# A gated linear-attention kernel with a two-matrix MLP: two tokens to a partition, one logarithm for both, quarter-tile scores and a written-out order

## The chip, the cores and the metric

The kernel runs on one core of a Trainium2 chip. A core has five engines that run beside each other and meet through semaphores: TensorE (PE, matrix products into PSUM), VectorE (DVE), ScalarE (ACT, functions from tables), GpSimd (POOL) and SyncE (SP), which here only issues transfers. Sixteen DMA engines move the data. PSUM has eight banks; only TensorE writes products to it, and VectorE and ScalarE read it.

The metric is the device time of one launch in microseconds. The kernel before takes 228.28 us (median of three runs, 227.02 to 230.74).

## The reference

For each of 4 batches and 8 heads a 48 x 48 state decays by a gate for each token and takes in an outer product. The outputs of the heads side by side, 3072 tokens of 384 numbers, then go through two matrices with a smooth gate between them:

```python
f = 1.0 / (1.0 + np.exp(-f_logit))
for t in range(S):                       # S = 768, head_dim 48
    state = f[:, :, t, :, None] * state + np.einsum('bhd,bhe->bhde', k[:, :, t], v[:, :, t])
    y[:, :, t] = np.einsum('bhd,bhde->bhe', q[:, :, t], state)
x = y.transpose(0, 2, 1, 3).reshape(3072, 384)
h = x @ w_in                             # 384 x 2048
g = 0.5 * (h + np.sqrt(h * h + 4.0))
out = g @ w_out                          # 2048 x 384
```

q, k, v, f_logit and the weights come as float32 in HBM, and the result is float32.

## The kernel before

The work goes in 24 chunks of 128 tokens, two chunks making a pair of 256 tokens; there are 12 pairs, three to a batch. A token is a partition. Each chunk is loaded by a transfer of its own, whose contiguous runs are the 48 floats of one token and head, 192 bytes:

```python
for r in range(x, y):                                   # the chunks of a pair
    nc.sync.dma_start(out=T[name, p][:, r],
        in_=src_of[name][b][:, c * C:(c + 1) * C, :].rearrange("h t d -> t h d"))
```

The product of gates up to a token is the exponential of a running sum. ScalarE takes exp(-f) and ln(1 + e), both over all 768 numbers of a partition (2 chunks x 8 heads x 48). The result is split into a high and a low half-precision part, TensorE sums both over the tokens with a triangular matrix `wcent`, and ScalarE takes two exponentials for each chunk. GpSimd or VectorE then multiplies q and k by them:

```python
nc.scalar.activation(out=f, in_=f, func=AF.Exp, scale=-1.0)                    # 128 x 768
nc.scalar.activation(out=T["ls", p][:, x:y], in_=..., func=AF.Ln, bias=1.0)    # 128 x 768
...                                                     # lhi = half(ls), llo = half(ls - lhi)
nc.tensor.matmul(out=ca, lhsT=wcent, rhs=lhi[...][:, r, :, 0:D], start=True, stop=False)
nc.tensor.matmul(out=ca, lhsT=wcent, rhs=llo[...][:, r, :, 0:D], start=False, stop=True)
...                                                     # sums at the chunk's ends: 16 small products
nc.scalar.activation(out=T[name, p][:, r]..., in_=T["ca", p, r][:, 0:H * D], func=AF.Exp, scale=sign)
eng.tensor_tensor(out=qk[...][:, x:y, i, :, 0:D], in0=T[name, p][:, x:y], in1=T[e, p][:, x:y], op=ALU.mult)
```

q and k are transposed for each chunk, by TensorE for pairs 0 to 4 and by the DMA for pairs 5 to 11. Scores, mask, output and state of a chunk follow:

```python
nc.tensor.matmul(out=T["sc", r, s][:, j, :], lhsT=qkT[o:o + D, NP + j, :], rhs=qkT[o:o + D, j, :],
                 start=True, stop=True)                 # 8 a chunk, 48 rows x 128 columns, over 128
nc.vector.tensor_tensor(out=T["pm", r][:, s], in0=T["sc", r, s], in1=mask16..., op=ALU.mult)
nc.tensor.matmul(out=y[:, j], lhsT=T["qkT", r][:, j, :], rhs=T["sn", r][:, j], ...)
nc.tensor.matmul(out=y[:, j, s], lhsT=T["pm", r][:, s, j, :], rhs=T["v16", p][:, i, 2 * j + s, :], ...)
...                                                     # state: u = old state + k^T v, then times gam
```

y is copied to half precision and transposed to `xT`. The MLP of a pair is 48 products of 256 columns (M1, into the tile hps) with a square, a root and a gate between them, and 32 products of 384 columns (M2, into o):

```python
nc.tensor.matmul(out=hb[:, a, :], lhsT=w_in16[j2][:, j, a * 128:(a + 1) * 128], rhs=T["xT", p][:, j, :], ...)
nc.scalar.activation(out=T["hsq", p, j4][:, a], in_=T["h", p, j2], func=AF.Square, scale=1.0)
nc.scalar.activation(out=T["r16", p, j4], in_=T["hsq", p, j4], func=AF.Sqrt, scale=0.25, bias=1.0)
nc.vector.scalar_tensor_tensor(out=T["g", p]..., in0=T["h", p, 2 * j4 + a], scalar=0.5, in1=T["r16", p, j4][:, a],
                               op0=ALU.mult, op1=ALU.add)
nc.tensor.matmul(out=T["o", p, i], lhsT=T["g", p][:, jn, i * C:(i + 1) * C], rhs=w_out16[jn // 2][:, jn % 2, :], ...)
nc.sync.dma_start(out=out[t0:t0 + C, :], in_=T["o_sb", p, i])
```

Exp and ln lie in one table of ScalarE and sqrt in another, so a change from one kind of work to the other loads a table. The order of all instructions is made at build time by a list scheduler (`Plan`) from priorities in the source. PSUM is split into three fixed rings: five banks for hps, two for everything of the attention, one for o. The copy of o leaves through a ring of two `o_sb` buffers.

Of the kernel before, what the change touches and what calls it, by code (L numbers as in the profile page):

```python
# [15 lines left out]
GROUPS = [[0], [1], [2], [3], [4], [5, 6], [7, 8], [9, 10], [11]]  # L16

XBAR = [5, 6, 7, 8, 9, 10, 11]

BASE = {  # L20
    "A": [-91.5, -48.2, -86.7, 59.5, 5.1, 3.6, 35.4, 93.4, 55.3, 161.2, 112.5, 128.2],
    "B": [-33.0, -23.9, 18.0, -28.5, -32.3, 71.1, -18.2, 43.6, 49.9, 25.6, 129.6, 106.7],
    "M": [63.0, -3.2, -1.9, 48.3, 21.6, 51.8, 114.9, 66.8, 229.7, 86.1, 210.4, 238.2],
    "O": [63.2, 45.4, 128.9, 46.1, 124.2, 143.7, 179.0, 123.5, 212.6, 237.4, 202.6, 191.4],
}
PART = {n: k for k, v in {
    "A": "W hi lo qk v16 nls gam", "B": "T SC KV Y Yc YT xq xy", "M": "M1 M R G", "O": "M2 ev out"}.items()
    for n in v.split()}

SHIFT = {  # L30
    "ld": 25.6, "win": 4.5, "wout": 7.0, "W": -4.7, "hi": 73.7, "lo": -32.1, "qk": -11.9, "v16": -32.1,
    "nls": -54.3, "gam": -112.9, "T": -87.4, "xq": -171.2, "SC": 9.3, "Y": -140.2, "Yc": 36.7, "YT": 70.6,
    "xy": 89.2, "KV": 58.5, "M1": 3.8, "M": 94.0, "R": -53.7, "G": -57.6, "M2": 33.2, "ev": -104.7,
    "out": 212.9,
}

NEAR = {'PE': 0.02, 'ACT': 0.1, 'DVE': 0.05, 'POOL': 0.3, 'SP': 0.2}

ENG = {
    "hi": "DDDDPDPPPPPP",  # L40
    "lo": "PPPDPPPDPPPD",
    "qk": "PPPPDPDDPDPP",
    "v16": "PDPPDPPPPPPP",
    "T": "DDADDDDDDDAAADDADDADDDDD",
    "Yc": "AADDADDDDDDDDDADDDDDDDDD",
    "ev": "DDDDDADDDDDDDADADAADAAAA",
}
FULL = {"D": "DVE", "A": "ACT", "P": "POOL"}

FINE = [0]  # L50

START = {"POOL": 3.8, "DVE": 3.6, "PE": 3.4, "ACT": 0.7, "SP": 0.7}

AFTER = {'in': 0, 'out': 2}


NH, NA, NO = 5, 2, 1

WDMA, VDMA = True, False

ORDER = "P0 P1 i03 f2 i47 o07 qkv2"


class Op:
    __slots__ = ("eng", "dur", "deps", "emit", "due", "allocs", "uses", "end", "kind", "dma", "ins", "flow", "issued")

    def __init__(self, eng, dur, emit, deps=(), due=0.0, allocs=(), uses=(), kind=None, dma=None, ins=()):
        self.eng, self.dur, self.emit, self.due, self.kind, self.dma = eng, dur, emit, due, kind, dma
        self.deps = [d for d in deps if d is not None]
        self.allocs, self.uses = list(allocs), list(uses)  # L70
        for b in self.uses:
            b.users.append(self)
        self.end = None
        self.ins = list(ins)
        self.flow = None


class Ring:
    def __init__(self, n, ordered):
        self.n, self.bufs, self.ordered, self.made = n, [], ordered, 0  # L80


class Buf:
    def __init__(self, ring):
        self.ring, self.users = ring, []
        self.seq = ring.made
        ring.made += 1


class Plan:  # L90

    HOP = 0.22
    TABLE = 1.3

    def __init__(self):
        self.queues = {}
        self.order = []

    def add(self, queue, eng, dur, emit, p=None, at=None, due=0.0, **kw):
        if isinstance(dur, dict):
            eng = FULL[ENG[queue][p if at is None else at]]
            dur = dur[eng]
        due += SHIFT.get(queue, 0.0) + (0.0 if p is None else BASE[PART[queue]][p])
        op = Op(eng, dur, emit, due=due, **kw)
        self.queues.setdefault((eng, queue), []).append(op)
        return op

    def ready(self, op):  # L110
        t = 0.0
        for d in op.deps:
            if d.end is None:
                return None
            t = max(t, d.end + (0.0 if d.eng == op.eng and d.dma is None else self.HOP))
        for b in op.allocs:
            r = b.ring
            k = len(r.bufs) - r.n
            if r.ordered and b.seq != len(r.bufs):
                return None  # L120

            k += sum(1 for x in op.allocs[:op.allocs.index(b)] if x.ring is r)
            if k >= 0:
                for u in r.bufs[k].users:
                    if u.end is None:
                        return None
                    t = max(t, u.end + (0.0 if u.eng == op.eng and u.dma is None else self.HOP))
        return t

    def flows(self):  # L130


        todo = {"SP": [], "POOL": []}
        for op in self.order:
            if not isinstance(op, str) and op.dma is not None:
                todo[op.eng].append([op.issued, op.dma[0], op])
        t = 0.0
        while todo["SP"] or todo["POOL"]:
            live = {e: q[0] for e, q in todo.items() if q and q[0][0] <= t + 1e-9}
            later = [q[0][0] for e, q in todo.items() if q and e not in live]  # L140
            if not live:
                t = min(later)
                continue
            rate = {"SP": 0.35, "POOL": 0.65} if len(live) == 2 else {e: 1.0 for e in live}
            step = min([x[1] / rate[e] for e, x in live.items()] + [a - t for a in later])
            t += step
            for e, x in live.items():
                x[1] -= step * rate[e]
                if x[1] <= 1e-9:
                    x[2].flow = t + x[2].dma[1] - x[2].issued  # L150
                    todo[e].pop(0)

    def run(self, passes=3):
        for n in range(passes):
            for ops in self.queues.values():
                for op in ops:
                    op.end = None
                    for b in op.uses + op.allocs:
                        b.ring.bufs = []
            self.order = []  # L160
            self.once()
            if n + 1 < passes:
                self.flows()

    def once(self):
        heads = {k: 0 for k in self.queues}
        free = dict(START)
        dma_free = 0.0
        table = None
        left = sum(len(v) for v in self.queues.values())  # L170
        by_eng = {}
        for k in self.queues:
            by_eng.setdefault(k[0], []).append(k)
        stretch = None
        loose = False
        while left:
            best = None
            for eng, ks in by_eng.items():
                now = free.get(eng, 0.0)
                cands = []  # L180
                for k in ks:
                    if heads[k] < len(self.queues[k]):
                        op = self.queues[k][heads[k]]
                        t = self.ready(op)
                        if t is not None:
                            cands.append((max(now, t), op, k))
                if not cands:
                    continue
                if eng == "PE" and stretch is not None and not loose:

                    if any(heads[k] < len(self.queues[k]) and self.queues[k][heads[k]].kind == ("W", stretch)
                           for k in ks):
                        cands = [c for c in cands if c[2][1] != "M1" or not c[1].allocs]
                        if not cands:
                            continue
                if eng == "ACT" and stretch is None and not loose:

                    opened = []
                    for c in cands:
                        if c[1].kind is not None and c[1].kind[0] == "W":  # L200
                            ins = [d for o in self.queues[c[2]][heads[c[2]]:heads[c[2]] + 16]
                                   if o.kind == c[1].kind for d in o.ins]
                            if any(d.end is None for d in ins):
                                continue
                            c = (max([c[0]] + [d.end - 1.0 for d in ins]),) + c[1:]
                        opened.append(c)
                    cands = opened
                    if not cands:
                        continue
                if eng == "ACT":  # L210

                    if stretch is not None and not loose:
                        mine = [c for c in cands if c[1].kind == ("W", stretch)]
# [662 lines left out]
```

## Time and profile before

| | before |
|---|---|
| time, median (range) | 228.28 us (227.02 to 230.74) |
| VectorE busy | 157.0 us (69%) |
| ScalarE busy | 168.7 us (74%) |
| GpSimd busy | 75.1 us (33%) |
| loads of f, q, k, v | 4 x 24 of 192 KB, 3.8 to 4.0 us to landing |
| first product of M1 | 24.16 us after the start |
| end of the last load's issue | about 140 us |

The profile is one execution, 228.4 us from the first instruction to the last. Its first part gives busy time by engine. Its second cuts the span into 40 slices of 5.7 us, where a digit is the busy share in tenths. Products on TensorE are pipelined and overlap, so the sum of their durations is more than the time they take; the distance from one start to the next is what one costs. Later parts list the transfer queues, the chain that ended last, and the groups of equal instructions. An idle time is put down to the instruction whose end released it.

### The profile page before, as it was taken

The page shows a single profiled execution, that of the slowest core. Times are in us where ns is not written, and L with a number is a line of the kernel's source. Part 1 is how long each engine was busy: PE and PEld are TensorE (multiplying, and loading weights), DVE is VectorE, ACT ScalarE, POOL GpSimd, SP SyncE. Part 2 cuts the span into 40 slices and gives each one's busy share as a digit, 9 for nine tenths or more (in the row PEclk, how much of TensorE's full clock was granted, in tenths as well). Part 3 has the DMA queues.
Part 4 walks back from the last instruction along what each step waited for, and adds up shares of the span by engine and source line. Part 5 has one row for each costly group of instructions (what it writes and reads, how often), then busy time and mean ns, then how long its engine had stood idle before and what let it go on. Part 6 is the DMA issues. An engine that isn't in the chain of part 4 may idle for free.

```text
span 228.4 us, 4796 instructions
## 1 busy us (share of the span) xinstructions
PE 186.2 (82%) x1870; PEld 133.3 (58%) x1870; DVE 157.0 (69%) x295; ACT 168.7 (74%) x258; POOL 75.1 (33%) x74
## 2 busy tenths in 40 slices
PE   0456858589998499599449999699999999999983
PEld 0243636357666257477326766576777777777641
DVE  6154286699895469598155998489989899855420
ACT  5333395999999918399705998599799999999820
POOL 5799426560640449610000692012504200000000
PEclk9999997999999589999967999999999999999999
DMA  7999999999998998999980569411193532010101
GB/s 140 207 194 188 178 208 181 204 155 202 189 222 170 230 209 175 247 171 220 220 207 1 124 139 207 102 52 55 52 195 76 119 47 57 17 54 34 70 34 69
DMA packets 129303, 32.10 MB, mean 141 GB/s; under 512 B 121088, under 2 KB 129280, under 8 KB 129280
## 3 DMA queue, kind: packets, MB, share of 16 engines
q1 hardware_dynamic: 123904, 28.65, 63.6%
q0 software_dynamic: 5376, 3.15, 9.5%
q8 instruction: 14, 0.23, 0.4%
q14 instruction: 9, 0.07, 0.1%
HBM read 25.17 MB, written 4.72 MB: 131 GB/s over the span
## 4 chain that ended last, share of the span: by engine, by line
PE 57%; ACT 16%; DVE 7%; DMA 6%; POOL 5%; SPq 4%; issue 3%; POOLq 0%; ACTq 0%; DVEq 0%
PE o L780 23%; PE hps L740 22%; ACT hsq L746 5%; DMA out_dram<-o_sb 4%; ACT r L755 4%; SPq L363 4%; PE sc L618 2%; DMA xT<-y 2%; DVE pm L625 2%; POOL w_in L388 2%; POOL qk L487 2%; PE hps L468 2%; ACT L843 2%; PE hps L467 1%; PE y L641 1%
## 5 line engine op out<-in xcount | busy, mean ns | idle before, releaser
L780 PE MATMUL o<-w_out,g 128*128 128x384 f16 x384 | 76.0, 335 | 14.7 <-DVE o_sb L791 13.5
L740 PE MATMUL hps<-xT,w_in 128*128 128x256 f16 x576 | 75.0, 282 | 3.7 <-DMA xT<-y 2.3
L763 DVE SCALAR_TENSOR_TENSOR g<-hps,r 128x512 f16<-128x512 f32 x96 | 61.6, 683 | 12.7 <-ACT r L755 12.3
L746 ACT ACTIVATE hsq<-hps 128x512 f16<-128x512 f32 x96 | 53.8, 591 | 22.0 <-PE hps L740 21.0
L740 PEld LDWEIGHTS <-w_in 128*128 128x128 f16 x576 | 56.7, 101 | 15.8 <-issue 5.0
L780 PEld LDWEIGHTS <-g 128*128 128x128 f16 x384 | 36.3, 100 | 34.8 <-issue 17.5
L755 ACT ACTIVATE r<-hsq 128x1024 f16<-128x1024 f16 x48 | 50.7, 1057 | 1.3
L625 DVE TENSOR_TENSOR pm<-sc,mask 128x512 f16<-128x512 f32 x48 | 31.1, 683 | 9.0 <-PE sc L618 9.0
L494 POOL CAST v<-ld_v 128x768 f16<-128x768 f32 (+1 forms) x11 | 8.5, 771 | 57.6 <-PE y L641 36.8
L487 POOL TENSOR_TENSOR qk<-ld_q,ea 128x768 f16<-128x768 f32 (+1 forms) x9 | 14.7, 1631 | 34.9 <-ACT ea L481 33.5
L481 ACT ACTIVATE ea<-hps 128x384 f32<-128x384 f32 x24 | 10.6, 491 | 12.1 <-PE hps L474 12.1
L791 DVE COPY o_sb<-o 128x384 f32<-128x384 f32 x15 | 8.3, 554 | 15.7 <-DMA out_dram<-o_sb 14.9
L436 POOL TENSOR_TENSOR llo<-ls,lhi 128x768 f16<-128x768 f32 (+1 forms) x10 | 15.3, 1534 | 9.8 <-DVE gam L547 6.2
L487 POOL TENSOR_TENSOR qk<-ld_k,eap 128x768 f16<-128x768 f32 (+1 forms) x9 | 15.4, 1712 | 0.0
L425 ACT ACTIVATE ld_f<-ld_f 128x768 f32<-128x768 f32 (+1 forms) x13 | 10.5, 804 | 4.6 <-DMA ld_f<-in_f_logit_dram 4.6
L467 PE MATMUL hps<-lhi,wcent 128*128 128x384 f16 x24 | 8.9, 370 | 5.8 <-DVE lhi L433 5.8
L618 PE MATMUL sc<-qkT 48*128 48x128 f16 x192 | 11.0, 228 | 2.4 <-DVE pm L625 1.1
L710 DVE TENSOR_TENSOR sn<-u,gam 128x384 f16<-128x384 f32 x20 | 11.0, 549 | 2.4 <-PE u L706 2.3
L641 PE MATMUL y<-v,pm 128*128 128x48 f16 x192 | 11.8, 187 | 0.4 <-DVE pm L625 0.4
L597 DVE COPY qkT<-tr 128x1024 f16<-128x1024 f16 x9 | 6.0, 685 | 8.7 <-PE tr L593 8.7
L641 PEld LDWEIGHTS <-pm 128*128 128x128 f16 x192 | 10.2, 99 | 3.0 <-issue 1.3
L618 PEld LDWEIGHTS <-qkT 48*128 48x128 f16 x192 | 6.2, 98 | 9.5 <-issue 8.0
(55 smaller groups left out, 217.5 us busy)
## 6 DMA issues: line engine op xcount, KB each, us to landing
ld_f<-in_f_logit_dram SPq DMA_DIRECT2D x24, 192.0 KB, 4.0
ld_q<-in_q_dram SPq DMA_DIRECT2D x24, 192.0 KB, 3.8
ld_k<-in_k_dram SPq DMA_DIRECT2D x24, 192.0 KB, 3.8
ld_v<-in_v_dram SPq DMA_DIRECT2D x24, 192.0 KB, 3.9
out_dram<-o_sb SPq DMA_DIRECT2D x24, 192.0 KB, 2.2
w_in<-in_moe_w_in_dram POOLq DMA_DIRECT2D x8, 192.0 KB, 7.7
w_out<-in_moe_w_out_dram POOLq DMA_DIRECT2D x8, 192.0 KB, 6.8
qkT<-qk SPq DMA_TRANSPOSE x14, 3.3
```

The costliest lines, as they stand in the source:

```text
L436: eng_of[lg[p, x].eng].tensor_tensor(out=llo[p % NL][:, x:y, :, 0:D], in0=T["ls", p][:, x:y], in1=lhi[p % NL][:, x:y, :, 0:D], op=ALU.subt ...
L467: nc.tensor.matmul(out=ca, lhsT=wcent, rhs=lhi[p % NL][:, r, :, 0:D], start=True, stop=False)
L487: eng_of[mu[p, x, i].eng].tensor_tensor(out=qk[p % NB][:, x:y, i, :, 0:D], in0=T[name, p][:, x:y], in1=T[e, p][:, x:y], op=ALU.mult)
L618: nc.tensor.matmul(out=T["sc", r, s][:, j, :], lhsT=qkT[o:o + D, NP + j, :], rhs=qkT[o:o + D, j, :], start=True, stop=True)
L625: nc.vector.tensor_tensor(out=T["pm", r][:, s], in0=T["sc", r, s], in1=mask16.unsqueeze(1).broadcast_to([128, NP, C]), op=ALU.mult)
L641: nc.tensor.matmul(out=y[:, j, s], lhsT=T["pm", r][:, s, j, :], rhs=T["v16", p][:, i, 2 * j + s, :], start=(c == 0), stop=(c == 0 or s == 1))
L710: nc.vector.tensor_tensor(out=T["sn", r + 1], in0=T["u", r], in1=gam[b % 2][:, c].unsqueeze(3).broadcast_to([128, NP, 2, D]), op=ALU.mult)
L740: nc.tensor.matmul(out=hb[:, a, :], lhsT=w_in16[j2][:, j, a * 128:(a + 1) * 128], rhs=T["xT", p][:, j, :], start=(j == 0), stop=(j == NJ - 1))
L746: nc.scalar.activation(out=T["hsq", p, j4][:, a], in_=T["h", p, j2], func=AF.Square, scale=1.0)
L755: nc.scalar.activation(out=T["r16", p, j4], in_=T["hsq", p, j4], func=AF.Sqrt, scale=0.25, bias=1.0)
L763: nc.vector.scalar_tensor_tensor(out=T["g", p][:, jn:jn + 2, :].rearrange("p a t -> p (a t)"), in0=T["h", p, 2 * j4 + a], scalar=0.5, in1= ...
L780: nc.tensor.matmul(out=T["o", p, i], lhsT=T["g", p][:, jn, i * C:(i + 1) * C], rhs=w_out16[jn // 2][:, jn % 2, :], start=(jn == 0), stop=( ...
```

## The change

Two neighbouring tokens now share a partition, so a chunk of 128 tokens is 64 partitions and a pair of 256 tokens fills all 128. A load brings a whole pair in runs of 2 x 48 floats, 384 bytes. With u = 1 + exp(-f) of both tokens and their product t, one logarithm of t serves both tokens; the running sums and their exponentials are those of token pairs, and what separates the two tokens is multiplied into q and k by VectorE or GpSimd. Scores run as products with 64 output rows on quarters of the array, transposes, state and output products with 64 rows of input. The rest of the MLP has the same instructions as before. The scheduler is replaced by a list of 1009 words in the source, which fixes the order, the engine of each movable operation, and the PSUM bank of each product; any bank may serve anything.

The core of the diff (cut; the removed `Plan` and the removed parts shown above are left out):

```diff
-GROUPS = [[0], [1], [2], [3], [4], [5, 6], [7, 8], [9, 10], [11]]
-XBAR = [5, 6, 7, 8, 9, 10, 11]
-NH, NA, NO = 5, 2, 1
+XBAR = [4, 5, 6, 7, 8, 9, 10, 11]
+DEPTH = {'f': 3, 'q': 3, 'k': 3, 'v': 3, ..., 'y16': 2, 'xT': 5, 'hsq': 2, 'r16': 2, 'g': 4, 'os': 2}
+ORDER = """
+lf0.0:S lf0.1:S lf1.0:S lk0.1:S lk0.0:S TABLE:e ex0.0:A lq0.1:S ut0.0:P ex0.1:A lq0.0:S tt0.0:D ...
+... m1.0.0:T@4 te1.1.0:D m1.0.2:T@6 te1.0.0:D sq0.0:A ut3.0:P m1.0.1:T@5 sb0:D ...
+... gt11.7:D m2.11.02:T ev10.0:D m2.11.03:T st10.01.0:S m2.11.11:T ev11.0:D st10.01.1:S ...
+"""
+ # loads: a pair of tokens to a partition
+ eng(e).dma_start(out=T[s, p][:, hs].rearrange("p h i d -> p h (i d)"),
+                  in_=src[s][bb][hs, t0:t0 + 256, :].rearrange("h (p i) d -> p h (i d)", i=2))
+ # u = 1 + exp(-f) of both tokens, t = u0 * u1, one logarithm
+ nc.scalar.activation(out=t, in_=t, func=AF.Exp, scale=-1.0)                      # 128 x 768
+ eng(e).tensor_scalar(out=T["UT", p][:, 0::2, hs], in0=..., scalar1=1.0, scalar2=None, op0=ALU.add)
+ mul(e, u[:, 1, hs], u[:, 0, hs], u[:, 2, hs])                                    # 128 x 384
+ nc.scalar.activation(out=T["s", p][:, hs], in_=T["UT", p][:, 1, hs], func=AF.Ln) # 128 x 384
+ # running sums before and up to the token pair: 2 x 2 products of 384 columns and 8 small ones a pair
+ nc.tensor.matmul(out=o, lhsT=K["tri"][:, m], rhs=hl[:, r, hs, 0:D], start=(r == 0), stop=(r == 1))
+ nc.scalar.activation(out=T[nm, p]..., in_=T["cum", p, m]..., func=AF.Exp, scale=sgn)   # once a pair for each
+ mul(e, t, t, T["UT", p][:, 2, hs])                     # qu: first token's q times u of the second, 384
+ mul(e, t, t, T["UT", p][:, 0:2, hs])                   # ku: both tokens' k times u and t, 768
+ for i in range(2):                                     # qm, km: two products of 384 each
+     mul(e, K["qk"][...][:, s, h0 // 2:h1 // 2, i, :, 0:D], T[nm, p][:, hs, i]..., T[en, p][:, hs]...)
+ # scores: 16 products for each of two key positions, 48 rows x 64 columns, over 128
+ nc.tensor.matmul(out=T["sc", p, i, h][64 * cc:64 * cc + 64, j, :],
+                  lhsT=t[r, 1, j, i, :], rhs=t[r, 0, j], start=True, stop=True)
+ # state and output: 64 rows of input, the old state added by a product with the identity
+ nc.tensor.matmul(out=T["u", p, cc][:, j], lhsT=K["qk"][...][r, 1, j, i]..., rhs=T["v16", p][r, 2*j:2*j+2, i, :], ...)
+ nc.tensor.matmul(out=T["y", p, cc][:, h, :], lhsT=T["pm", p, i, h % 2][r, h // 2, :], rhs=T["v16", p][r, h, i, :], ...)
+ # stores: a pair leaves in two transfers, one for each of the two token positions
+ eng(e).dma_start(out=out[t0:t0 + 128 * n, :].rearrange("(c u i) d -> i u c d", c=n, i=2)[i],
+                  in_=T["os", p][64 * i:64 * i + 64, c:c + n])
+ for word in ORDER.split():
+     ...
+     W.pieces[name].emit(e or W.pieces[name].eng, banks)
```

In a word of the list, `m1.0.2:T@6` is part 2 of M1 of pair 0 on TensorE into bank 6; S, P, D and A stand for SyncE, GpSimd, VectorE and ScalarE, and TABLE for a table load. By the words, ScalarE loads a table 10 times (16 before). ScalarE takes 13 of 24 copies of y and 13 of 24 copies of o (4 and 9 before). The DMA transposes 8 pairs (7 before).

## The prediction

> **What bounds the kernel now.** I read the page's busy shares and slices first, then cut the span where the transfers let up, then asked for the waits and the chain there.
>
> ```profile
> PE 186.2 (82%) x1870; PEld 133.3 (58%) x1870; DVE 157.0 (69%) x295; ACT 168.7 (74%) x258; POOL 75.1 (33%) x74
> PE   0456858589998499599449999699999999999983
> DMA  7999999999998998999980569411193532010101
> DMA packets 129303, 32.10 MB, mean 141 GB/s; under 512 B 121088, under 2 KB 129280, under 8 KB 129280
> q1 hardware_dynamic: 123904, 28.65, 63.6%
> ```
>
> No engine is full over the span, but the DMA row is full or nearly so for the first 21 slices, and in those PE is ragged; behind them PE shows nines. So there are two stages. The windows divide it at 120 us (columns: PE, PEld, DVE, ACT and POOL busy, clock, DMA share, GB/s; the second fence has PE and PEld of M1 alone):
>
> ```profile
> 0.00:120.00 120.00, 84.88 (x862) 60.20 (x863) 78.56 (x159) 81.93 (x127) 55.58 (x60) 0.94 1.08 196
> 120.00:228.40 108.40, 101.36 (x1009) 73.07 (x1007) 78.46 (x137) 86.77 (x131) 19.53 (x14) 0.99 0.36 79
> ```
> ```profile
> 0.00:120.00 120.00, 30.79 (x228) 23.10 (x229) 0.94 1.08 196
> 120.00:228.40 108.40, 44.24 (x348) 33.55 (x347) 0.99 0.36 79
> ```
>
> In 120 us only 228 of 576 M1 products are done, in the last 108 us 348. The first stage belongs to the transfers. What they do to the engines is in the waits and in the chain between 70 and 100 us:
>
> ```profile
> DVE o_sb L791 <- DMA out_dram<-o_sb: 14.9, 3, 7.1
> PE o L780 <- DVE o_sb L791: 13.5, 4, 6.2
> ACT hsq L746 <- PE hps L740: 21.0, 17, 8.8
> ```
> ```profile
> 71.94 0.70 SPq L363
> ...
> 73.50 3.24 DMA out_dram<-o_sb
> 76.78 0.04 issue
> 76.82 0.57 DVE o_sb L791
> 77.39 0.04 issue
> 77.43 1.44 PE o L780 x4
> ```
>
> SP's queue is in order: a store stands behind load issues that crawl because the transfers are behind; its buffer is late, the copy of o waits, and the single o bank stops M2. That is 13.5 us on PE.
>
> **What the Trainium skill says.** (1) "DMA: Bandwidth & Descriptors", Specifications: full rate needs at least 512 bytes a transfer piece, of a ceiling of 435 GB/s. The trace agrees in direction: from 8 to 14 us, with loads almost alone, 192-byte pieces moved 203 GB/s at a share of 1.04. (2) "ScalarE: Activation LUTs", What ACT_TABLE_LOAD costs: about 1283 ns whatever the set. The trace has 1283 ns for each of 16. (3) "TensorEngine Tiling (Array Packing)", Key Properties: tiles of the array work independently, but a change of tiling mode drains it. Nothing in this trace tests it. (4) "VectorE: DVE Perf Modes", The perf-mode tier table: a float32 product of two tensors has only the basic rate. The trace agrees: 956 ns for 768 elements.
>
> **Loads.** 18.87 MB at 203 GB/s are 93 us now. A 192-byte piece holds one DMA engine for 192 x 16 / 203 = 15 ns. Were that all fixed cost, 384-byte pieces would take 46 us; were it all bytes, 93. I choose 75 us (250 GB/s), nearer to the upper end, because from 18 to 30 us, where weights in pieces of 1024 bytes (256 floats) mix in, the rate is 186 GB/s and no higher. That is 18 us of transfers less, nearly all in the first stage. SP issues 52 loads in place of 96 (about 0.75 us each before). Weights, transposes and stores keep their bytes.
>
> **ScalarE.** Exponentials: 48 of 0.50 us become 24, in equal counting minus 9 to 12; I take 10. Logarithms: 768 elements at 0.844 become 384 at about 0.50, minus 4.1. Table loads: 6 x 1.283 = minus 7.7. Added: 9 copies of y (0.478) plus 4.3, 4 of o (0.473) plus 1.9, small copies and casts about plus 4.5. Net minus 11. Square and root (96 x 0.565 and 48 x 1.057, 105 us) stay, so ScalarE keeps about 158 us.
>
> **VectorE and GpSimd.** The 96 gates (0.683), 48 masks (0.683) and 20 state products (0.549) stay, 109 us. The rest of VectorE's words, at the rows' durations for their sizes, makes about 48: it stays at 157. GpSimd gets u, the products with it and most of q and k: by its words 12 of about 1.85 us, 14 of 2.0, 9 of 0.93, 10 casts of 0.83, 10 sums of 0.85, 16 weight issues of 0.78 and smaller ones, together 103 us where it had 75. It has the room.
>
> **TensorE by pitch, not by duration.** M1: 48 groups of 12 at 1.31 us, 63 us. M2: 96 groups of 4 at 0.65, 62 us. Unchanged, 125. The attention now costs about 46: sums 12 x 1.07, transposes 80 x 0.057, scores 192 x 0.057, outputs 24 x 0.40, states 20 x 0.32, second transposes 10 x 0.17. After: sums 12 x 0.86 (half of the small ones at 0.027 go), 10; transposes 3; scores 384 quarters, of which two abreast would cost 10.9 and four abreast 5.5: I take 8 for drains; outputs 11; states 8; second transposes 2. That is 42, and 167 in all, 4 less. So the change hardly shortens TensorE's work; it can gain only from keeping it fed.
>
> **Sum by stage.** I counted the list's words between five marks and multiplied by the durations above. Until the first M1: before at 24.16 us. After, chain and transfers through pair 0's f, k, q and v (seven pair loads, 11 us, plus 2.5 us until the first lands), then cast, masks, output, copy, transpose: 20. From there to the third pair's first M1 words: TensorE 30, ScalarE 35, VectorE 34, transfers 37: 37. To the sixth pair: 45.5, 46, 44, transfers 41.5: 46. To the ninth: 34, 32.5, 30: 34. To the last M1 word: 44.5, 36, 31: 44.5. Rest: 13 quarters of M2, 9, and copy and store, 3. Together 193.5. That supposes perfect packing. In the second and third stage three engines and the transfers tie within a few us, and a fixed order lets each wait for the others: I add 12% of 83, 10 us; in the later ones TensorE leads alone and I add nothing, as it had next to no gaps there before. Total 203 us.
>
> **Rivals.** *The order is brittle.* Every bank and engine follows one list; a late load holds SP, then GpSimd, then all. For it: the wait of 8.8 us on M1 above came from such a chain, and buffers for loads go from four or three to three. Against it: any bank may serve o now and a pair has its own output buffer. Two or three stalls like the two on the stores would give 212 to 220 us. *TensorE takes the place of the transfers early.* If quarter and half tiles run one after the other or each of some 100 mode changes drains for 0.15 us, the attention costs 55 to 60 in place of 42: 214 to 218 us. Nothing in the trace speaks either way. *Longer pieces pay in full.* If the piece is mostly fixed cost, transfers leave the second and third stage to ScalarE and the engines pack better: 193 to 196 us. *Hidden anyway.* If the first stage were held by the attention's chain and not by transfers, only the 4 us of the start would come: 223. Full DMA slices next to ragged PE ones speak against it.
>
> **Range and chances.** The first rival in half measure gives 210, the third 195; I widen to 193 to 216. Faster by over 2% means below 223.7; only two rivals together reach it. Faster 0.91, within 2% 0.05, slower 0.04.
>
> **What would show it.** The loads' mean rate in the first 15 us should be near 250 GB/s. The DMA row should come down from its nines by about 100 us, not 120. M1 should start near 20 us and half of M1 be done before 105 us. The wait of the copy of o on a store should be below 4 us. ScalarE should show 10 table loads and some 158 us, GpSimd about 100. TensorE's slices should read nine from about the twelfth on; the start-to-start distance of score products tells two or four abreast. The prediction falls if PE's gaps stay ragged through the middle with the DMA row low, or if small products on PE take over 55 us.

## The result and the profile after

| | before | after |
|---|---|---|
| median (range) of 5 runs each | 228.16 us (226.43 to 230.74) | 219.87 us (219.4 to 221.5) |
| ratio, 95% interval | 1 | 0.9661, 0.9605 to 0.9718 |

The kernel is 3.4% faster, where 11% were predicted. 219.87 us lies above the range of 193 to 216. So the direction was right and some 17 us of the sum are to be found.

The page of the kernel after, its first three parts (an engine's busy time and share, 40 slices of 5.5 us in tenths, transfers):

```profile
PE 183.4 (83%) x2320; PEld 130.2 (59%) x2320; DVE 162.9 (74%) x284; ACT 155.3 (71%) x252; POOL 118.4 (54%) x128
PE   0348948869589999976995799999989999999991
POOL 6899477299975966889999902939000000000002
PEclk9999996999999999999999658999999999999998
DMA  6999999089980989999969797981991017102204
DMA packets 82073, 32.87 MB, mean 150 GB/s; under 512 B 73952, under 2 KB 82000, under 8 KB 82048
q1 hardware_dynamic: 76528, 29.07, 65.5%
```

Two rows are to be read one above the other. GpSimd (POOL), at a third of the span before, is at 118.4 us. It has its nines in slices 9 to 11 and again in 19 to 23, with eights in front. TensorE dips to 6 and 5 in slices 9 and 11 and again to 7, 6, 9, 9, 5, 7 in slices 18 to 23, and at the end of the second dip the granted clock falls as well (6, 5, 8 in slices 23 to 25). GpSimd's busy time alone would have passed for harmless: 54%.

The next table shows where the time lies by stages. They are cut at the starts of M1's product groups 1, 17, 41, 64 and 96 (six products each), the marks of the prediction. The first row is the prediction's stage sum without its allowance, the others are differences of start times in one trace each, so that their last digits need not add up; the lower two kernels come from the experiments below:

| us | start | 2 | 3 | 4 | 5 | rest | sum |
|---|---|---|---|---|---|---|---|
| predicted, perfect packing | 20 | 37 | 46 | 34 | 44.5 | 12 | 193.5 |
| after | 24.1 | 44.2 | 48.7 | 43.5 | 45.2 | 13.9 | 219.7 |
| addition on VectorE (u_dve) | 22.8 | 40.9 | 47.8 | 37.7 | 45.4 | 13.8 | 208.4 |
| also stripped of most of GpSimd's products and of loads (u_dve_bare) | 23.8 | 38.2 | 45.6 | 35.1 | 44.1 | 13.5 | 200.3 |

Stages 2 and 3 are 7.2 and 2.7 us over, about the 10 us allowed for them. What else is over is in stage 4 (9.5 us), for which nothing had been allowed, in the start (4.1), and 2.6 in the last two.

What delayed the work of stage 4, which begins at 117 us, is in the chain of waits of the kernel after between 88 and 128 us (start, duration, what; "issue" is time without a visible wait):

```profile
88.77 1.03 POOL k L136
89.80 0.74 issue
90.54 1.33 POOL q L136
91.87 2.41 POOL UT L182
94.28 0.20 POOL gs L136
94.47 2.10 POOL UT L182
96.60 1.62 DVE UT L136 x2
...
113.66 0.74 ACT f L175
...
115.57 2.14 POOL UT L182
117.73 1.34 DVE UT L136
119.07 1.07 DVE hl L133
...
123.73 2.16 DVE qk L136
```

In the middle, from 102 to 113 us (left out above), the chain runs through TensorE, which leads elsewhere. Before and behind that its largest part is GpSimd's line L182. That is the addition u = 1 + exp(-f), in pairs 8 and 9 first and pair 11 later. Behind it hang the product t, the logarithm, the sums, the exponentials, the scaled q and k, and last the scores. The groups of GpSimd's instructions in the kernel after, shapes kept apart (busy us, mean ns, idle before and its releasers):

```profile
L182 POOL TENSOR_SCALAR UT<-f 128x768 f32<-128x768 f32 x9 | 20.1, 2238 | 7.0 <-ACT f L175 3.7 <-issue 3.1
L136 POOL TENSOR_TENSOR k<-k,UT 128x768 f32<-128x768 f32 x10 | 18.5, 1855 | 2.6 <-DVE g L465 2.6
```

An addition of a constant to 768 numbers takes 2.24 us, longer than the product of two tensors of that size, 1.86. The prediction had 0.85 for it, next to 0.83 for a cast of that size.

The waits of the kernel after (us in total, times, longest) show what was gained and what came in its place:

```profile
ACT s L196 <- DVE UT L136: 8.3, 6, 3.1
DVE UT L136 <- POOL UT L182: 6.6, 5, 2.4
...
PEld L440 <- DMA win<-in_moe_w_in_dram: 4.8, 3, 3.5
...
PE ps L477 <- DMA wout<-in_moe_w_out_dram: 2.7, 3, 1.5
...
ACT os L131 <- DMA out_dram<-os: 0.7, 1, 0.7
```

The copy of o waits 0.7 us on a store (14.9 before). But now there are waits on u and t, and waits on weights, whose transfers GpSimd issues in the same list.

### The profile page after: what moved, and what is told of

It reads as the page before. It is cut to its first block, busy times and chain, and to the rows that moved or that the text cites. A ratio compares the mean times of both kernels' runs of the same rounds, so it can differ in the third digit from the quotient of the medians.

```text
span 219.7 us, 5661 instructions
## 1 busy us (share of the span) xinstructions
PE 183.4 (83%) x2320; PEld 130.2 (59%) x2320; DVE 162.9 (74%) x284; ACT 155.3 (71%) x252; POOL 118.4 (54%) x128
## 4 chain that ended last, share of the span: by engine, by line
PE 44%; DVE 15%; POOL 12%; ACT 11%; DMA 10%; issue 4%; SPq 2%; POOLq 0%; DVEq 0%
PE ps L440 18%; PE ps L477 18%; POOL UT L182 6%; DMA wout<-in_moe_w_out_dram 4%; ACT r L455 3%; DMA win<-in_moe_w_in_dram 3%; DVE qk L136 3%; DVE UT L136 3%; DVE q L136 3%; ACT hsq L449 3%; DMA qkT<-qk 2%; PE ps L334 2%; DVE pm L341 2%; POOL wout L145 2%; ACT f L175 2%
## 5 line engine op out<-in xcount | busy, mean ns | idle before, releaser
L440 PE MATMUL ps<-xT,win 128*128 128x256 f16 x576 | 75.3, 282 | 7.0 <-DVE g L465 3.2
L465 DVE SCALAR_TENSOR_TENSOR g<-ps,r 128x512 f16<-128x512 f32 x96 | 62.2, 683 | 20.8 <-ACT r L455 20.6
L477 PE MATMUL ps<-wout,g 128*128 128x384 f16 x384 | 72.4, 330 | 2.8 <-DMA wout<-in_moe_w_out_dram 2.7
L440 PEld LDWEIGHTS <-win 128*128 128x128 f16 x576 | 56.7, 101 | 19.9 <-DMA win<-in_moe_w_in_dram 4.8
L449 ACT ACTIVATE hsq<-ps 128x512 f16<-128x512 f32 x96 | 53.9, 595 | 19.0 <-PE ps L440 18.3
L477 PEld LDWEIGHTS <-g 128*128 128x128 f16 x384 | 36.7, 99 | 24.1 <-issue 4.5
L341 DVE TENSOR_TENSOR pm<-ps,mask 128x512 f16<-128x512 f32 x48 | 30.9, 680 | 8.2 <-PE ps L334 8.2
L182 POOL TENSOR_SCALAR UT<-f 128x768 f32<-128x768 f32 (+1 forms) x10 | 21.3, 2132 | 8.0 <-ACT f L175 4.6
L136 POOL TENSOR_TENSOR k<-k,UT 128x768 f32<-128x768 f32 (+1 forms) x12 | 21.1, 1763 | 2.6 <-DVE g L465 2.6
L221 PE MATMUL ps<-hl,tri 128*128 128x384 f16 (+1 forms) x52 | 12.2, 349 | 9.9 <-POOL hl L133 6.5
L136 POOL TENSOR_TENSOR qk<-q,ea 128x384 f16<-128x384 f32 (+1 forms) x16 | 15.7, 1005 | 0.2
L221 PEld LDWEIGHTS <-tri 128*128 128x128 f16 x52 | 5.2, 104 | 13.7 <-issue 5.4
```

Of the source, the lines that this page charges most:

```text
L136: eng(e).tensor_tensor(out=o, in0=a, in1=b, op=ALU.mult)
L182: eng(e).tensor_scalar(out=T["UT", p][:, 0::2, hs], in0=T["f", p][:, hs].rearrange("p h i d -> p i h d"), scalar1=1.0, scalar2=None, op0=A ...
L221: nc.tensor.matmul(out=o, lhsT=K["tri"][:, m], rhs=hl[:, r, hs, 0:D], start=(r == 0), stop=(r == 1))
L341: nc.vector.tensor_tensor(out=T["pm", p, i, h], in0=T["sc", p, i, h], in1=K["mask"][:, i].unsqueeze(1).broadcast_to([128, 4, 128]), op=ALU ...
L440: nc.tensor.matmul(out=T["h", p, m][:, a], lhsT=K["win"][m][:, j, a * 128:(a + 1) * 128], rhs=T["xT", p][:, :, j, :], start=(j == 0), stop ...
L449: nc.scalar.activation(out=T["hsq", p, r][:, a], in_=T["h", p, m].rearrange("p a c t -> p (a c t)"), func=AF.Square, scale=1.0)
```

## The theories and the experiments

The theory: the addition on GpSimd costs 2.2 us where 0.85 were reckoned. That fills GpSimd's in-order list, and u, the weights and q and k come late. Its rivals: the weights' transfers are late by themselves; the two-input products of GpSimd and VectorE hold each other up; the written order is brittle, whatever an operation costs.

Ratios are to the kernel before, run on the same chip at the same time: four executions of each kernel (17 of runs192) beside 7 or 20 of the kernel before. Compare ratios, as the median of the kernel before itself was 227.26 to 230.28 us in these groups. Executions over 1.5% above the fastest of their kernel are left out of a ratio but not of the median beside it: in u_dve and u_dve_pcopy these are two of four, and the medians without them are 209.71 and 207.48 us. A point below is 1% of the time of the kernel before, 2.3 us.

| run | what is changed against after | median us | ratio, 95% interval |
|---|---|---|---|
| u_copy | addition becomes a copy | 213.81 | 0.9406, 0.9361 to 0.9452 |
| u_dve | addition on VectorE | 211.35 | 0.9223, 0.9164 to 0.9282 |
| u_act | addition on ScalarE | 211.48 | 0.9302, 0.9265 to 0.9340 |
| u_mix | addition half on each of these | 212.19 | 0.9344, 0.9298 to 0.9391 |
| w_one | one weight tile of each kind | 215.16 | 0.9444, 0.9380 to 0.9508 |
| u_dve_w | u_dve, weights issued earlier | 211.92 | 0.9232, 0.9185 to 0.9278 |
| u_dve_wone | u_dve, one weight tile | 211.51 | 0.9230, 0.9196 to 0.9265 |
| u_dve_pcopy | u_dve, most of GpSimd's products become copies | 209.35 | 0.9063, 0.9007 to 0.9119 |
| u_dve_v3 | u_dve, 9 of 12 pairs' loads of v left out | 208.94 | 0.9176, 0.9117 to 0.9236 |
| u_dve_pcopy_v3 | both of these | 205.23 | 0.8944, 0.8890 to 0.8998 |
| u_dve_bare | both, and one weight tile | 201.62 | 0.8876, 0.8839 to 0.8914 |
| runs192 | loads cut into 192-byte runs | 226.88 | 0.9921, 0.9893 to 0.9950 |

### What the addition costs: u_copy

The same access pattern, the same engine and the same place in the list, without the arithmetic. The run leaves out the + 1; the exponent's scale is changed so that the logarithm stays in range.

```diff
-nc.scalar.activation(out=t, in_=t, func=AF.Exp, scale=-1.0)
+nc.scalar.activation(out=t, in_=t, func=AF.Exp, scale=0.05)
-eng(e).tensor_scalar(out=T["UT", p][:, 0::2, hs], in0=..., scalar1=1.0, scalar2=None, op0=ALU.add)
+eng(e).tensor_copy(out=T["UT", p][:, 0::2, hs], in_=...)
```

Expected:

> GpSimd forms u = 1 + exp(-f) by a copy in the place of the addition, in the same slots of the list (the +1 is left out and the exponent scaled by 0.05 so that the numbers keep their range). Theory A, GpSimd's list is the hidden bound from 28 to 64 and 84 to 127 us and the addition of 2.24 us for 0.85 is what overfilled it: the copy takes about 0.85 us, GpSimd's busy time falls from 118 to about 104 us, and the time from 219.9 to 206 to 212 us. Theory B, late weights hold the start and the rest is a brittle order: 216 to 219 us. If the copy still takes over 1.9 us, it is the access pattern and not the operation, and this run tells nothing of the time.

Measured: 213.81 us, 0.9406, which lies between the two forecasts, near the first. The group of the same line in this run:

```profile
L182 POOL COPY UT<-f 128x768 f32<-128x768 f32 x9 | 7.6, 849 | 11.0 <-issue 6.4 <-ACT f L175 3.6 <-DVE k L136 0.9
```

849 ns against 2238: the strided write is not what is dear, the addition is. The nine fall from 20.1 to 7.6 us, GpSimd's busy time from 118.4 to 106.0, and the time by 2.6 points, about 6 us. So about half of what is taken from this one line comes off the end of the kernel. M1 began 2.0 us later here than in the kernel after (26.1 us); that was not taken apart.

### The addition on another engine: u_dve, u_act, u_mix

Nothing is left out here. Ten of thirteen words of the list are changed in their letter (`u_dve`; the other three were VectorE's already), or all thirteen (`u_act`); in `u_mix` pairs 0 to 5 go to VectorE, 6 to 11 to ScalarE.

```diff
-... ut0.0:P ... ut2.0:P ... ut3.0:P ... ut8.0:P ... ut11.0:P
+... ut0.0:D ... ut2.0:D ... ut3.0:D ... ut8.0:D ... ut11.0:D
 # u_act: ut*:A, with
+if e == "A":
+    nc.scalar.activation(out=..., in_=..., func=AF.Identity, bias=1.0, scale=1.0)
```

Expected of `u_dve`:

> All 13 forming of u go to VectorE (0.62 us each), in the same slots; nothing is left out. Theory A: GpSimd about 98 us, VectorE about 168 us, and less waiting of VectorE on the shared reads; time 206 to 213 us. Theory B (weights, brittle order): 216 to 220 us, for VectorE's list only gets longer.

Expected of `u_act`:

> All 13 forming of u go to ScalarE, right behind the exponential it follows from (about 0.85 us each, 11 us more on an engine with 155 of 220 busy). Theory A: GpSimd about 98 us and one hop between engines less at each pair; 205 to 212 us. Theory B: 217 to 222 us.

Expected of `u_mix`:

> Nothing left out: u of pairs 0 to 5 on VectorE, of 6 to 11 on ScalarE, because VectorE is busy 45.7 of 47.8 us in the third stage and ScalarE 42.6. If that stage is held by VectorE: 208 to 210 us; otherwise as u_dve and u_act, 211 to 212 us.

Measured: 0.9223, 0.9302 and 0.9344. The page of the kernel with the addition on VectorE:

```profile
PE 179.4 (86%) x2320; PEld 128.4 (62%) x2320; DVE 162.4 (78%) x294; ACT 155.1 (74%) x252; POOL 99.1 (48%) x118
PE   0349974979899899998999899799979999999991
PEclk9999999799999999999999999999999999999997
```

The dip in the middle is gone, in PE and in the clock. The windows from 110 to 130 us, first of the kernel after, then of this one (columns: PE, PEld, DVE, ACT and POOL busy with counts, clock, DMA share, GB/s):

```profile
110.00:120.00 10.00, 7.92 (x141) 5.30 (x138) 6.50 (x9) 6.65 (x15) 9.74 (x8) 1.00 0.85 136
120.00:130.00 10.00, 7.87 (x85) 4.21 (x86) 8.70 (x14) 5.73 (x13) 5.95 (x6) 0.64 0.84 141
```
```profile
110.00:120.00 10.00, 9.20 (x159) 6.13 (x158) 10.00 (x18) 7.23 (x18) 7.22 (x8) 1.00 1.14 169
120.00:130.00 10.00, 10.00 (x139) 7.55 (x138) 8.34 (x14) 8.53 (x14) 1.55 (x2) 1.00 1.10 206
```

With the addition on GpSimd, TensorE ran 226 products in these 20 us, and GpSimd was at 9.74 of 10 in the first half; with it on VectorE, 298. Two engines with quite different loads receive the addition and the gain is much the same (4.4 and 3.6 points), so it comes from what GpSimd is rid of, not from where the work goes. Both runs lie in the range forecast for this theory. The mix was a miss: spreading the load further bought nothing. None of the three intervals touches that of the kernel after (0.9605 to 0.9718), so each of them beats both kernels. Which of `u_dve` and `u_act` is better is not shown, as their intervals overlap.

One number of the page of `u_dve` needs explaining. VectorE took over ten additions (11 of the large size, 7.5 us by its groups, stand there in place of 2 with 1.2), and yet its busy time fell from 162.9 to 162.4 us. The other products became shorter. The product qu on VectorE, in the kernel after and then with the addition on VectorE:

```profile
L136 DVE TENSOR_TENSOR q<-q,UT 128x384 f32<-128x384 f32 x2 | 4.2, 2100 | 0.0
```
```profile
L136 DVE TENSOR_TENSOR q<-q,UT 128x384 f32<-128x384 f32 x2 | 1.2, 614 | 0.0
```

The Trainium skill, "SBUF — State Buffer", Who interferes with whom, says that a VectorE instruction with two SBUF inputs contends with a GpSimd instruction that reads SBUF, because its second input comes through a shared read interface. The traces agree: in the kernel after, the km products of 384 numbers took 0.55 us on average in the four cases beside an idle GpSimd and 1.16 in the six beside a working one, though two of these six, beside one small product, took no more than 0.56 and 0.58. In `w_one` a qu product shows it plainly; the timelines of VectorE and of GpSimd in that run:

```profile
15.80 3.15 DVE L136 TENSOR_TENSOR q<-q,UT 128x384 f32<-128x384 f32 x1
```
```profile
15.77 0.99 POOL L136 TENSOR_TENSOR UT<-UT 128x384 f32<-128x384 f32 x1
16.72 1.80 POOL L136 TENSOR_TENSOR k<-k,UT 128x768 f32<-128x768 f32 x1
```

VectorE's instruction starts 0.03 us behind GpSimd's first one and ends at 18.95 us, 0.43 us behind the end of the second. Against the 0.61 us of this product in `u_dve`, most of its 3.15 us must be waiting, and the profile counts it as busy. Why it had to wait for the second as well, before which it had started, is not shown.

### Are the weights late by themselves: w_one, u_dve_w, u_dve_wone

`w_one` and `u_dve_wone` load one tile of each matrix and use it for all groups, so they leave out 14 of 16 weight loads; `u_dve_w` leaves nothing out and only issues them earlier.

```diff
 # w_one, u_dve_wone
-K["win"][m] ... K["wout"][jn // 2]      # words wi1 to wi7, wo1 to wo7
+K["win"][0] ... K["wout"][0]            # removed
 # u_dve_w: wi6, wi7 moved behind wi5; wo1 to wo7 moved behind vc2.0
```

Expected of `w_one`:

> One tile of each weight matrix is loaded and used for all groups (leaves out 14 of 16 weight loads: 14 issues of 0.78 us on GpSimd and their transfers). Theory B, weights hold the start: the waits of 4.8 and 2.7 us on them go and so does the contention with the loads, 205 to 211 us. Theory A: GpSimd is freed of 11 us in the first 53 us only, and the stretch from 84 to 127 us stays as it is; 212 to 216 us.

Expected of `u_dve_w`:

> u on VectorE as before in u_dve, and the weight loads moved ahead in GpSimd's list: win 6 and 7 right behind 5, wout 1 to 7 right behind 0, where GpSimd sat idle; nothing is left out. If late weight issues are what still holds the second stage (the chain there runs through a weight landing at 36 and one at 57 us), the third pair's first M1 group starts at about 59 us in place of 63.6, and the time is 206 to 209 us against 211.4. If the transfers are full there anyway and the weights only push the loads aside: 210 to 214 us.

Expected of `u_dve_wone`:

> u on VectorE, and one tile of each weight matrix loaded and used for all groups (leaves out 14 weight loads and their issues). The most that any better placing of the weights could bring: 203 to 206 us if the weights hold the second stage, 208 to 211 us if the rest is the engines packing imperfectly.

With the addition on GpSimd, the weights' issues and bytes are worth 2.2 points, about 5 us, as forecast for the theory, and stage 4 still takes 42.4 us. With the addition on VectorE they are worth nothing: 0.9230 and 0.9232 against 0.9223. Issued earlier, they did not bring the third pair's M1 forward either: it began at 65.6 us, 63.6 in `u_dve`. The times of `u_dve_w` and `u_dve_wone` lie in or next to the second of their forecasts. The waits on weights do not vanish with the addition: in `u_dve`, TensorE's weight loads still wait 5.0 us for them. But removing them gains nothing there. So the 5 us of `w_one` are best read as relief for GpSimd's list, which is rid of 14 issues of 0.74 to 0.82 us; that the bytes had no part in it is not shown. A rival that saves time alone and nothing once the main cause is gone is no second cause of that loss.

### What the rest is made of: u_dve_pcopy, u_dve_v3, u_dve_pcopy_v3, u_dve_bare

3.3 points, about 7.5 us, lie between `u_dve` and the predicted 0.889. Two suspects are left: GpSimd's products with what they do to VectorE's, and the transfers. The first edit makes copies of GpSimd's products where its test on the shapes lets it, so it leaves the factors out there. Contrary to the expectation below it does not reach the largest ones: the twelve ku products keep their factors, because the test excludes their shape (ten of 1.82 us in the stripped run), as do the subtractions for the low half. The second edit leaves out the loads of v of pairs 3 to 11 and casts the first three pairs' buffers again.

```diff
 def mul(e, o, a, b):
+    if e == "P" and tuple(o.shape) == tuple(a.shape) and o.shape[1] > 3:     # pcopy
+        nc.gpsimd.tensor_copy(out=o, in_=a)
+        return
-func=AF.Exp, scale=sgn
+func=AF.Exp, scale=0.1 * sgn
-copy(e, T["v16", p][:, hs], T["v", p][:, hs])                                # v3; words lv3 to lv11 removed
+copy(e, T["v16", p][:, hs], T["v", p % 3][:, hs])
```

Expected of `u_dve_pcopy`:

> u on VectorE, and every product that GpSimd makes replaced by a copy of its first input (leaves the factors out; the exponents are scaled to a tenth to keep the range). If GpSimd's products, and VectorE's waiting beside them, are still a bound in the middle: GpSimd about 65 us, VectorE's products of 384 elements back at 0.55 us, time 201 to 206 us. If TensorE, ScalarE and the order bound it now: 208 to 211 us.

Expected of `u_dve_v3`:

> u on VectorE, and v of pairs 3 to 11 not loaded but cast again from the first three pairs' buffers (leaves out 9 of 12 v loads, 3.5 MB or about 13.5 us of transfers, all before 125 us of the run, and GpSimd's waits of 13.5 us on them). If the transfers are again what holds the kernel once GpSimd is relieved: 203 to 207 us. If not, 209 to 212 us.

Expected of `u_dve_bare`:

> Everything at once on u_dve: 14 weight loads and 9 v loads left out, and GpSimd's products made copies. Alone the first brought nothing and the last 2 us. If GpSimd and the transfers cover for each other, so that either alone hides the other: 198 to 204 us. If TensorE, ScalarE and VectorE in their fixed order set the rest: 207 to 210 us.

Expected of `u_dve_pcopy_v3`:

> As u_dve_bare, but with all weights loaded: GpSimd's products are copies and 9 v loads are left out. Which transfers hide behind GpSimd? If those of the middle (v beside q, k, f): 202 to 205 us. If the weights of the start: 206 to 209 us.

In points of the ratio below `u_dve`: products 1.6, loads of v 0.5 (this interval overlaps with that of `u_dve`, so it is no clear gain by itself), both 2.8, both with one weight tile 3.5. Of the times, those of the products alone and of the loads alone lie between their two forecasts or at the edge of the second, and that of `u_dve_pcopy_v3` at the edge of its first; only `u_dve_bare` is clearly within one, 198 to 204 us. Neither suspect carries the rest alone. That each hides the other is suggested by 2.8 being more than 1.6 + 0.5, but the difference is within the intervals. GpSimd's products do lengthen VectorE's work: with the loads of v left out, VectorE is busy 163.8 us beside the products and 154.9 beside the copies (`u_dve_v3` and `u_dve_pcopy_v3`). The page of the stripped kernel, `u_dve_bare`:

```profile
PE 178.1 (89%) x2320; PEld 128.7 (64%) x2320; DVE 157.5 (79%) x294; ACT 155.0 (77%) x252; POOL 67.5 (34%) x104
PE   0437896879999999999999989999999999999991
```

TensorE reads 9 from the tenth slice on, with one 8. Its stages 3 to 5 take 45.6, 35.1 and 44.1 us where 45.5, 34 and 44.5 had been counted for TensorE. So the sum for the leading engine held; the kernel with the addition moved does not reach it because GpSimd's products and the transfers, taken together, stand in the way. A remainder of the start, 3.8 us, stays even here and was not taken apart.

### What the longer runs are worth: runs192

Each load is cut into two of 192-byte runs, one for each token of the pair; where the data lies and all computation stay. It also doubles SP's load issues, 52 to 104, so the two are changed together.

```diff
-eng(e).dma_start(out=T[s, p][:, hs].rearrange("p h i d -> p h (i d)"), in_=src...)
+for i in range(2):
+    eng(e).dma_start(out=T[s, p][:, hs, i], in_=src[s][bb][hs, t0:t0 + 256, :].rearrange("h (p i) d -> i p h d", i=2)[i])
```

Expected:

> The changed kernel with its loads cut in two, so that a contiguous run is 192 bytes again and there are 104 load issues in place of 52; the layout on the chip is unchanged. If the transfers still pace the first half, the loads run near 205 GB/s in place of 260 and the time is 226 to 233 us. If GpSimd has taken their place as the bound, most of that is hidden: 220 to 224 us.

Measured: 0.9921, so 2.6 points, about 6 of the 8 us gained, are given back. The window from 2 to 15 us, of the kernel after and of this run:

```profile
2.00:15.00 13.00, 3.30 (x49) 2.47 (x49) 10.80 (x28) 5.52 (x14) 10.82 (x15) 1.00 1.20 263
```
```profile
2.00:15.00 13.00, 3.16 (x48) 2.43 (x48) 9.93 (x28) 5.53 (x14) 8.60 (x14) 1.00 1.00 192
```

263 GB/s against 192, with full queues both times (shares of 1.20 and 1.00). Part of the 192 may be due to the issues: SP issues quarters of pair 0 of 98 KB at 0.55 us each here, which allows no more than 179 GB/s. The kernel before, with runs of 192 bytes too and 192 KB to an issue, moved 210 GB/s in this window. So shorter runs and more issues together give back most of the gain, and their shares were not separated; what is left of the change, as it is written, brought 0.8% on balance. The loss is in stage 3, 56.1 us for 48.7. Stage 2 took 42.3 for 44.2, so slower loads cost nothing there in these two traces.

## Why the prediction was wrong

**Failed: "It has the room."** This is the step, and in it the term "10 sums of 0.85". The additions took 21.3 us (nine of 2.24, one smaller) in place of 8.5; that is 12.8 of the 15.4 us by which GpSimd's 118.4 exceeded the 103 of the sum. The durations for its other words were near (ku 1.86, predicted 1.85; qu 1.07, predicted 0.93). No row of the profile before showed an addition of a constant of that size on GpSimd; the row nearest to the figure is the cast's, 0.83, and the text did not mark it as borrowed. The changed source has it too: the entry for this operation is `"P": 0.19 + 0.86e-3 * 2 * n`, 0.85 us for n = 384, so whoever wrote out the order seems to have reckoned with the same. That last is a reading of the source, not a run. The conclusion failed with the term. Even 118 us in 220 look like room, but they are not spread: from 42 to 64 us GpSimd is busy 21.5 of 22 us, from 84 to 127 us 38.0 of 43, and in-order engines wait behind it. Moving the addition takes back 4.4 of the 7.7 points between the measured ratio and the predicted 203 / 228.28 = 0.889.

**Failed with it: "in the later ones TensorE leads alone and I add nothing".** The backlog of GpSimd spilled into stage 4, 43.5 us for 34. With the addition moved it is 37.7, stripped 35.1. What the full list delayed was paid a stage later. That the allowance of 10 us for stages 2 and 3 came out in size is luck: it was meant for three engines and the transfers waiting for one another, but stripped of GpSimd's surplus and of loads these stages are only 0.8 us over the count (38.2 and 45.6 for 37 and 46).

**Mis-sized: VectorE "at the rows' durations".** 162.9 us for 157, and the miss is larger than that. The prediction's 109 us for gates, masks and states multiplies mean durations, which overlap; the same rows are busy 103.7 us before and 104.1 after. So the rest took 58.8 us where 48 were reckoned. Its two-input products take longer beside a working GpSimd, as shown above. The products of GpSimd, with what they do to VectorE's, and the transfers are the other part of the miss: 3.5 points from `u_dve` to the stripped kernel, and they could not be separated further.

**Right.** Loads: 263 GB/s from 2 to 15 us, predicted 250 (229 over the whole first 15 us, in which nothing has landed at first). ScalarE: 155.3 us, predicted 158, with ten table loads. The copy of o on a store: 0.7 us, predicted below 4. TensorE's own work by stage, as the stripped kernel shows. And scores that run side by side on the array; in the timeline of TensorE, 32 quarter products of the kernel after, then 8 half ones of the kernel before:

```profile
27.73 0.64 PE L334 MATMUL ps<-qkT 48*64 48x128 f16 x32
```
```profile
89.53 0.40 PE L618 MATMUL sc<-qkT 48*128 48x128 f16 x8
```

These times include the 0.22 us that the last product of each takes. From start to start, the quarters come four within some 10 ns and the next four 56 ns later, 13.7 ns each: four abreast, for which the prediction reckoned 5.5 us in all before it chose 8. But in the kernel before the halves start in twos, 3 to 4 ns apart, and the next two 56 ns later. So the prediction's "scores 192 x 0.057" put them at twice their cost, its "Nothing in this trace tests it" overlooked that tiles already ran side by side, and the scores cost TensorE about the same as before, some 5.4 us (56 ns for each four of 384, or two of 192). The rival "TensorE takes the place of the transfers early" fell.

**Half right.** M1 started at 24.1 us, as before (24.16), and not at 20. In the kernel after, VectorE's qu product of pair 1 stretched to 2.40 us ahead of the masks; with the addition moved the product took 0.68 us and M1 began at 22.8. The DMA row comes down from its solid nines at about 110 us, but with gaps it goes on to about 165. The mark "half of M1 be done before 105 us" was wrong in itself: the prediction's own sum puts the start of the sixth pair at 113 us with its allowance. The 49th of 96 groups started at 137.6 us after, 124.3 with the addition moved. TensorE's nines "from about the twelfth" slice broke off in slices 18 to 23; in the stripped kernel they hold.

**The rivals.** "The order is brittle" gave 212 to 220, and the time fell there, but by a stall of another kind: not a late load that holds SP, but one operation that is dearer than the order assumes. The same order, with that operation on another engine, runs at 210 to 212. "Longer pieces pay in full" fell: 263 GB/s, where full pay would be twice 203. "Hidden anyway" fell: the shorter runs and their issues gave back 2.6 points.

**Open.** The DMA's transposes of q and k landed in a median of 4.6 us, 3.3 before, and stand in the chain of `u_dve`'s fourth stage with 4.86 us once. No run was made on it. Whether another order would win the rest back was not tried either.

## What to carry to other kernels

Before work is moved to an engine that "has the room", look for a row of that very operation on that engine; a cast does not stand for an addition. Then lay the work out by stages: an in-order engine at half load over the span can be nearly full for 40 us, and the bill comes a stage later on another engine. And when several late things are issued by one engine, take the load off that engine first and ask after the others again.

## What the runs showed of the hardware

- GpSimd, 768 float32 numbers on 128 partitions: addition of a constant 2.24 us on average (2.12 to 2.50), copy in the same access pattern 0.85, product of two tensors 1.86. The one-input arithmetic was the slowest of the three.
- VectorE's two-input products of 384 numbers took about 0.55 us beside an idle GpSimd, 1.16 on average (km) and 3.15 once (qu) beside a working one, and this counts as busy in the profile. In `u_dve` VectorE made ten more additions at no more busy time (162.4 us for 162.9); in `u_dve_w`, with the same additions, it was busy 166.3.
- Scores of 48 x 64 quarters over 128 columns ran four abreast on TensorE, 13.7 ns from start to start, and 48 x 128 halves two abreast, 26 ns.
- After TensorE had been short of work from 110 us on, its granted clock was 0.64 over the next 10 us; with the addition moved it stayed at 1.00 in the same 20 us. In the slices a 4 of TensorE in the sixth is followed by a clock of 6 in the seventh too, but the 5 in the eleventh by a full clock. So a gap may cost more than its length; that was not tested by itself.
